# Block 0 of a fused attention and feed-forward kernel: the third chunk's hidden product by one level of Strassen's method, and block 0 in a plan of slots

## The chip, the cores and the metric

The kernel runs on one core of a Trainium2 chip. A core has TensorE (PE, matrix products; its weight loads, PEld, overlap them), VectorE (DVE), ScalarE (ACT), GpSimd (POOL) and SyncE (SP, which here only issues DMA transfers). Each engine works through its own queue in order and waits on semaphores. Matrix products land in PSUM, in banks; everything else works in SBUF. All data here is float32, except that the two weight matrices arrive as float64 and are rounded to float32 on the chip.

The metric is the device time of one execution in microseconds; lower is better. Several runs of the same kernel lie within about 0.15% of each other.

## The reference

```python
kv = np.einsum('bhsd,bhse->bhde', k, v)          # batch 8, heads 8, seq 576, head_dim 64
out = np.einsum('bhsd,bhde->bhse', q, kv)
rms = np.sqrt(np.mean(out * out, axis=-1, keepdims=True) + 1e-06)
attn = (out / rms * g_norm).astype(np.float32)
x = attn.transpose(0, 2, 1, 3).reshape(B * S, H * D)   # 4608 x 512
h = x @ w_in                                     # w_in 512 x 2048
g = np.maximum(0.01 * h, h)
return (g @ w_out).astype(np.float32)            # w_out 2048 x 512
```

## The kernel before

**Blocks and chunks.** The 4608 rows of x are worked on in nine blocks of 512. The 2048 hidden columns come as four chunks (c = 0 to 3) of 512. For each chunk a block computes h = x · w_in (an h product), applies the leaky ReLU to get g, and adds g · w_out to the block's outputs (an o product). Attention for the following block is computed between them.

**Strassen.** A product of 512 x 512 by 512 x 512 taken in halves needs eight quarter products; Strassen's method (in Winograd's form) makes it with seven, and sums of quarters before and after them. `strassen` (line 923) yields after each of the seven, in the order 1, 2, 6, 5, 7, 3, 4. Each has four matrix products of 128x256 columns; on TensorE each of these is two instructions. Products 1, 6, 7 and 4 run in one PSUM bank, 2, 5 and 3 in a second; products 1, 2 and 5 open their bank anew, the others add to what is there, after the engine that read the last state is done. `product_h` (line 995) does this for h: ScalarE copies products 1, 5 and 6 out, VectorE adds products 2, 3 and 7, ScalarE applies the ReLU to each finished quarter, from PSUM for product 4. The sums on the side of w_in are s5, s6 (first pair) and s7, s3 (second pair), made by `sides_w1` (line 776); those on the side of x are t1 to t4, where t3 overwrites a quarter of x. Later blocks use two levels.

**Block 0** is in `first_block` (line 1431). Before the change its chunks 0, 1 and 2 go by plain h products (`plain_h`: per 128 hidden rows four matrix products of 512 columns, in banks ha and hc by turns), and only chunk 3 by one level of Strassen. The outputs of chunks 0 to 2 are plain (`plain_o`, a unit being one 128-row part of one left factor) and collect in four banks of PSUM, which ScalarE copies to SBUF at the end of the block (line 1532). The h product of a chunk stands beside the o products of the chunk before it. The o products of chunk 3 run in block 1.

**Weights.** The 32 weight pieces ("jobs" 0 to 31, 512 KB each as float64) are loaded by SP into seven buffers by turns (`load_w`) and rounded (`round_on`): two conversions on ScalarE, a clamp, a shift, a merge and a final add on VectorE. For jobs in `SIGNED` ScalarE makes the sign part, and VectorE's shift falls away. A job's last steps are issued with the next job's first ones (`end_w`). Before, jobs 0 to 3 are w_in of chunk 0, then w_in of chunk 1 and w_out of chunk 0 take turns, then w_in of chunk 2 and w_out of chunk 1, then w_in of chunk 3, w_out of chunk 2 and of chunk 3.

**Order.** While block 0 is built, nearly all instructions are pinned in program order (`pin`, `lined`); `ROUND_0`, `ROUND_1`, `ROUND_3`, `A_1`, `A_3`, `TAIL_1`, `X_1`, `S_1` and `UNITS` (lines 1422 to 1429) say after which step how many jobs are rounded, which steps of the attention of batch 1 go on, and where sums stand. GpSimd makes block 1's first sums of w_in (`sides_w1(0)`, behind a one-element copy at line 1520 that waits for job 31) and the sums of the fourth chunk's w_out (`sides_w2`, lines 797 to 818). In block 1 `combine` (line 832) makes second-level sums of w_in, parts 0 and 1 on GpSimd and part 2 on VectorE, in the tile `stage`.

Of the kernel before, what the change touches and what calls it, by code (L numbers as in the profile page):

```python
# [25 lines left out]
def kernel(  # L26
# [36 lines left out]
    nc = tc.nc  # L63
# [11 lines left out]
    U = 2  # L75
# [94 lines left out]
    def load_pair(b, p, what="kvq"):  # L170


        if "k" in what:
            k_ins[b, p] = load_two(nc.sync, k[b, 2 * p:2 * p + 2], in_tile("k"))
        if "v" in what:
            v_ins[b, p] = load_two(nc.sync, v[b, 2 * p:2 * p + 2], in_tile("v"))
        if "q" not in what:
            return
        t = q_tile(b, p)
        for l in range(2):  # L180
            for c in range(2):
                r0, n = 64 * l + 32 * c, T * D - 32 * c
                src = q[b, 2 * p + half_of(p, l)].rearrange("(t s) d -> t (s d)", s=T)
                pin(nc.sync.dma_start(t[r0:r0 + 32, :n], src[:, 32 * c:]))
        q_ins[b, p] = t
# [113 lines left out]
    for c in range(NC):  # L299
        for h in range(2):  # L300
            for u in range(U):
# [2 lines left out]
                           (w2_rows(h, c, u), w_out[f0:f0 + P].rearrange("p (v n) -> p v n", v=1 + h))]  # L304

    w_jobs = [w_jobs[8 * c + 2 * i + second] for stage_ in
              (((0, 0),), ((0, 1), (1, 0)), ((0, 2), (1, 1)), ((0, 3),), ((1, 2),), ((1, 3),))
              for i in range(2 * U) for second, c in stage_]
    w_raws = {}
    halved = [j for j, (_, src) in enumerate(w_jobs) if src.shape[1:] == (2, N2)]  # L310
# [16 lines left out]
            pass  # L327

    half_way = collections.deque()
    SIGNED = range(6, len(w_jobs), 2)  # L330

    def end_w():
        while half_way:
# [425 lines left out]

    more_all = consts.tile([P, 19 * P], F32, name="more")  # L760
    more = view(more_all, 0, 19, P)
    later, tick = [], -7

    def put_off(n, what):
        later.append((tick + n, what))
# [2 lines left out]
    def add(eng, out_, a, b_, minus=False, pinned=False):  # L768
        ins = eng.tensor_tensor(out_, a, b_, op=ALU.subtract if minus else ALU.add)  # L769
        if pinned or steady or in_first:  # L770
            pin(ins)
# [1 line left out]
    def w1_sums(c, i):  # L773
        return pair(i, U, 2, 2, P) if c and not in_first else view(more_all, i * NW, U, 2, 2, P)

    def sides_w1(c, eng=nc.gpsimd):


        a11, a12 = w1_sb[0][c][:, :, :2, :], w1_sb[0][c][:, :, 2:, :]
        a21, a22 = w1_sb[1][c][:, :, :2, :], w1_sb[1][c][:, :, 2:, :]  # L780
        s12 = w1_sums(c, 0)
        sides = {1: a11, 2: a12, 4: a22, 5: s12[:, :, :, 0, :], 6: s12[:, :, :, 1, :]}
        add(eng, sides[5], a21, a22)
        add(eng, sides[6], sides[5], a11, True)

        def more():
            s34 = w1_sums(c, 1)
            sides.update({7: s34[:, :, :, 0, :], 3: s34[:, :, :, 1, :]})
            add(eng, sides[7], a11, a21, True)
            add(eng, sides[3], a12, sides[6], True)  # L790
        return sides, more

    w2_dram = [[dram.tile([P, 2, U, N2], F32, name=f"w2_{c}_{i}") for i in range(2)]
# [576 lines left out]
    def go(steps, n=None):  # L1370
        while n is None or n > 0:
            if next(steps, steps) is steps:
                return
            n = None if n is None else n - 1
# [28 lines left out]
    def round_to(n):  # L1403
        nonlocal loaded, rounded
        while rounded < n:
            if loaded < len(w_jobs):
                load_w(loaded)
                loaded += 1
                if loaded in PAIR_AT:
                    load_pair(1, PAIR_AT[loaded])  # L1410
            round_on(rounded)
            rounded += 1
        if n == len(w_jobs):
            end_w()
# [4 lines left out]
        while later and later[0][0] <= tick:  # L1419
            later.pop(0)[1]()  # L1420

    ROUND_0 = 5, 6, 8, 9
    ROUND_1 = 11, 12, 14, 15, 17, 18, 19, 20, 21, 22, 24, 25, 26, 27, 28, 29
    ROUND_3 = 30, 31, 32
    TAIL_1 = 2, 3, 4
    A_1 = 5, 6, 8, 9, 10, 11, 12, 13, 14
    A_3 = 0, 1, 3, 4, 5, 5, 6
    X_1, S_1 = 12, 14
    UNITS = 2, 2, 2, 3, 2, 3, 2

    def first_block():
        x = xTs.pop(0)
        b11, b12 = x[:, :2, :N2], x[:, :2, N2:]
        b21, b22 = x[:, 2:, :N2], x[:, 2:, N2:]
        t1, t2, t4 = xt1[0], xt24[0][:, 0], xt24[0][:, 1]
        lefts = [], [], []

        def plain_h(c, n):
            h, u = divmod(n, U)
            h_ps = ps_m.tile([P, NT], F32, tag=("ha", "hc")[n % 2], name="h_ps")  # L1440
            parts = 2 if c == n == 0 else 1
            for part in range(parts):
                cols = slice(part * NT // parts, (part + 1) * NT // parts)
                for e in range(NE):
                    matmul(h_ps[:, cols], lhsT=w1_sb[h][c][:, u, e, :], rhs=x[:, e, cols],
                           start=(e == 0 and part == 0), stop=(e == NE - 1), skip_group_check=True)
            gT = view(g_all[c % 2], n * NT, NT)
            lefts[c].append([gT[:, t * P:t * P + P] for t in range(4)])
            return lambda: pin(nc.scalar.activation(gT, h_ps, func=AF.Prelu, alpha=SLOPE))

        accs = [ps_m.tile([P, DM], F32, tag=t, name="o_acc") for t in ("oa", "oc", "hb", "hd")]
        os = dict(zip(("11", "21", "12", "22"), o_homes))
        quarters = o_all.rearrange("p (i u n) -> p i u n", i=4, u=2)

        take = []

        def plain_o(c):
            for n, left in enumerate(lefts[c]):
                h, u = divmod(n, U)
                right = w2_rows(h, c, u)  # L1460
                end = c == NC - 2 and n == 2 * U - 1
                for t in range(4):
                    for v in range(1 + h):
                        cols = slice(v * N2, v * N2 + N2) if h else slice(0, NT)
                        matmul(accs[t][:, cols], lhsT=left[t], rhs=right[:, v, :],
                               start=(c == 0 and n == 0), stop=end, skip_group_check=True)
                    if end:
                        to = quarters[:, t // 2::2, t % 2, :]
                        part = accs[t].rearrange("p (v n) -> p v n", v=2)
                        take.append((nc.scalar.copy, to, part))  # L1470
                    yield

        for n in range(2 * U):
            relu_h = plain_h(0, n)
            round_to(ROUND_0[n])
            relu_h()
        tail = tail_of(0, NT, S)
        a_steps = attention(1, False)
        x_adds = (t1, b12, b11, True), (t2, b22, t1, True), (b12, b22, b12, True), (t4, b21, t2, True)
        for c in range(1, NC - 1):  # L1480
            o_steps = plain_o(c - 1)
            for n in range(2 * U):
                for half in range(2):
                    at = 4 * U * (c - 1) + 2 * n + half
                    if half:
                        go(o_steps, 4)
                    else:
                        relu_h = plain_h(c, n)
                    round_to(ROUND_1[at])
                    if not half:  # L1490
                        relu_h()
                    if at in TAIL_1:
                        go(tail, 1)
                    if at in A_1:
                        go(a_steps, 1)
                    if at == X_1:
                        for x_add in x_adds[:2]:
                            add(nc.vector, *x_add)
                    if at == S_1:
                        w_sides, more_h = sides_w1(NC - 1, nc.vector)  # L1500
        x_sides = {1: b11, 2: b21, 3: b22, 4: t4, 5: t1, 6: t2, 7: b12}
        o_steps = plain_o(NC - 2)
        g_sides = {}
        h_steps = product_h(-1, w_sides, x_sides, g_sides)
        for t in range(7):
            later_steps()
            if t < len(ROUND_3):
                round_to(ROUND_3[t])
            go(h_steps, 1)
            if t == 0:  # L1510
                for x_add in x_adds[2:]:
                    add(nc.vector, *x_add)
                more_h()
            go(o_steps, UNITS[t])
            go(a_steps, A_3.count(t))
            if t == 2:
                for p in range(2):
                    load_pair(2, p)
            elif t == 3:
                pin(nc.gpsimd.tensor_copy(more_all[:1, :1], w2_1[:1, 1, NC - 1, U - 1, :1]))  # L1520
                next_sides, more_h = sides_w1(0)
            elif t == 5:
                for i in range(2):
                    sides_w2(-1)[1](i)
                next_x, _, sums, _ = sides_x(1)
                go(sums, 2)
            elif t == 6:
                go(sums)
        more_h()
        go(h_steps)  # L1530
        for copy, to, part in take:
            pin(copy(to, part))
        o_queue.append(product_o(-1, g_sides, os, store(0)))
        return next_sides, next_x
# [173 lines left out]
```

## Time and profile before

| | us |
|---|---|
| median of 3 runs | 905.16 (904.28 to 905.49) |
| the profiled execution | 904.45 |
| its span on the core | 902.7 |
| block 0's h and o products on TensorE, first to last | 22.29 to 122.80 |
| of these, third chunk's h beside the second's o | 65.81 to 95.83 |

Every date in the text is in microseconds from the start of the span. In a line of a timeline stand start, length, engine, line, operation, output and input tiles, count, and in brackets how long the engine had been idle and what ended that. In the chain of waits each line has start, length and the work that the end of the execution hung on. Tiles appear by shortened names: `w_all` is the home of w_in, `w` those of w_out, `pairs`, `more` and `stage` are working space, `xt` the sums on the side of x. Nearly all matrix products carry line 128 and nearly all additions line 769, so they are told apart by tiles.

### The profile page before, as it was taken

To read this page: it belongs to the slowest core of one execution; us is meant where nothing else is said; L and a number is where in the kernel's file an instruction comes from. 1 tells how busy PE (TensorE), PEld (TensorE's weight loads), DVE (VectorE), ACT (ScalarE), POOL (GpSimd) and SP (SyncE) were. 2 spreads that over 40 slices of the span, in tenths; PEclk is the share of its full clock that TensorE was granted. 3 is DMA by queue.
4 is the path that set the end of the run, shared out by engine and by line. 5 is a ranking of instruction groups with operands and counts; after the bars stand their busy time and mean duration, and the time that the engine had idled before them with its cause. 6 is when DMAs were issued, how large, how long until landed. Compare 5 with 4: busy or idle time off the path is not lost.

```text
span 902.7 us, 19186 instructions
## 1 busy us (share of the span) xinstructions
PE 896.1 (99%) x7376; PEld 796.5 (88%) x7376; DVE 620.0 (69%) x947; ACT 340.0 (38%) x661; POOL 529.0 (59%) x675
## 2 busy tenths in 40 slices
PE   9999999999999999999999999999999999999998
PEld 5555688888998999999999999999999999999997
DVE  6988798376675667685967498666876684646453
ACT  5755532232244432434343433343244324222420
POOL 2000189877438774776657584758486847783730
PEclk9999999999999999999999999999999999999999
DMA  8979139967989688968897788858886778677731
GB/s 302 310 232 326 48 116 287 321 241 252 277 281 336 194 273 262 312 206 277 241 313 277 234 278 270 319 176 263 255 279 184 233 217 269 203 234 233 252 118 52
DMA packets 109820, 220.07 MB, mean 244 GB/s; under 512 B 11296, under 2 KB 51616, under 8 KB 109728
## 3 DMA queue, kind: packets, MB, share of 16 engines
q1 hardware_dynamic: 105296, 213.26, 74.3%
q10 hardware_dynamic: 3984, 4.39, 1.4%
q8 instruction: 59, 0.97, 0.4%
q0 software_dynamic: 448, 1.18, 0.3%
q14 instruction: 33, 0.27, 0.1%
HBM read 188.38 MB, written 30.41 MB: 242 GB/s over the span
## 4 chain that ended last, share of the span: by engine, by line
PE 94%; POOL 2%; DMA 1%; DVE 1%; issue 1%; ACT 0%; DVEq 0%; POOLq 0%; ACTq 0%
PE o_a L128 20%; PE o_c L128 16%; PE h_hd L128 10%; PE h_ha L128 9%; PE h_hc L128 9%; PE h_hb L128 9%; PE o_acc L128 5%; PE h_ps L128 5%; PE o_ps L128 3%; PE h_a L128 2%; PE h_c L128 2%; PE h_b L128 2%; PE h_d L128 1%; PE kv_ps L128 1%; DMA pairs<-in_v_dram 1%; POOL more L769 1%
## 5 line engine op out<-in xcount | busy, mean ns | idle before, releaser
L769 POOL TENSOR_TENSOR gs<-g 128x512 f32<-128x512 f32 x64 | 88.0, 1376 | 128.5 <-ACT g L962 61.5
L769 DVE TENSOR_TENSOR o_all<-o_c,o_all 128x256 f32<-128x256 f32 (+1 forms) x128 | 72.1, 563 | 62.3 <-PE o_c L128 47.0
L128 PE MATMUL o_a<-pairs,gs 128*128 128x256 f32 x480 | 113.8, 379 | 0.0
L962 ACT ACTIVATE g<-g 128x512 f32<-128x512 f32 x127 | 77.7, 631 | 75.4 <-DVE g L769 75.3
L769 POOL TENSOR_TENSOR w_all<-w_all 128x512 f32<-128x512 f32 x28 | 49.7, 1775 | 87.1 <-ACT w_all L1184 86.9
L769 DVE TENSOR_TENSOR g<-g,w_all 128x512 f32<-128x512 f32 (+1 forms) x84 | 88.7, 1056 | 14.6 <-POOL w_all L769 8.8
L128 PEld LDWEIGHTS o_a<-pairs,gs 128*128 128x128 f32 x480 | 87.0, 190 | 9.7 <-DVE o_all L769 0.2
L769 POOL TENSOR_TENSOR pairs<-w_all 128x512 f32<-128x512 f32 x6 | 7.9, 1324 | 108.2 <-ACT cut L367 100.6
L769 DVE TENSOR_TENSOR w_all<-h_ha,w_all 128x512 f32<-128x512 f32 x42 | 28.7, 684 | 54.8 <-PE h_ha L128 53.0
L128 PE MATMUL o_c<-pairs,gs 128*128 128x256 f32 x280 | 66.2, 379 | 0.0
L769 DVE TENSOR_TENSOR o_all<-o_a,o_all 128x512 f32<-128x512 f32 (+1 forms) x56 | 37.5, 670 | 39.5 <-PE o_a L128 38.8
L1184 ACT COPY w_all<-h_hc 128x512 f32<-128x512 f32 x42 | 24.8, 591 | 104.2 <-PE h_hc L128 103.9
L1184 ACT COPY w_all<-h_ha 128x512 f32<-128x512 f32 x42 | 24.7, 588 | 104.4 <-PE h_ha L128 104.4
L128 PE MATMUL o_a<-w,g 128*128 128x256 f32 x256 | 60.7, 379 | 0.0
L128 PEld LDWEIGHTS o_c<-pairs,gs 128*128 128x128 f32 x280 | 51.0, 190 | 5.7
L769 DVE TENSOR_TENSOR g<-w_all 128x1024 f32<-128x1024 f32 x28 | 34.9, 1248 | 29.3 <-ACT w_all L1184 29.3
L128 PEld LDWEIGHTS o_a<-w,g 128*128 128x128 f32 x256 | 46.5, 190 | 5.2
L769 POOL TENSOR_TENSOR gs<-gs,g 128x512 f32<-128x512 f32 x32 | 43.8, 1368 | 2.2
L128 PE MATMUL h_hc<-stage,w_all 128*128 128x128 f32 x336 | 44.9, 276 | 0.0
L128 PEld LDWEIGHTS h_ha<-stage,w_all 128*128 128x128 f32 x336 | 43.1, 192 | 1.8 <-POOL xT L769 0.3
L128 PE MATMUL h_ha<-stage,w_all 128*128 128x128 f32 x336 | 44.4, 275 | 0.0
L128 PE MATMUL o_acc<-w,g 128*128 128x256 f32 (+1 forms) x144 | 44.2, 453 | 0.0
(329 smaller groups left out, 2413.8 us busy)
## 6 DMA issues: line engine op xcount, KB each, us to landing
w_all<-w SPq DMA_DIRECT2D x196, 448.0 KB, 4.7
pairs<-w SPq DMA_DIRECT2D x94, 256.0 KB, 4.3
w<-w SPq DMA_DIRECT2D x22, 448.0 KB, 5.4
v_in<-in_v_dram SPq DMA_DIRECT2D x29, 288.0 KB, 5.8
k_in<-in_k_dram SPq DMA_DIRECT2D x28, 288.0 KB, 5.0
q_in<-in_q_dram SPq DMA_DIRECT2D x46, 144.0 KB, 4.8
q_in<-in_q_dram SPq DMA_DIRECT2D x46, 140.0 KB, 4.9
w<-stage SPq DMA_DIRECT2D x12, 512.0 KB, 3.9
```

The source lines that it names most:

```text
L128: pin(nc.tensor.matmul(*args, **kw))
L769: ins = eng.tensor_tensor(out_, a, b_, op=ALU.subtract if minus else ALU.add)
L962: lined(nc.scalar.activation(t, t if src is None else src, func=AF.Prelu, alpha=SLOPE))
L1184: nc.scalar.copy(q[:, at], bank)
```

## The change

The third chunk's h (c = 2) goes by one level of Strassen's method too, by the same `product_h`, beside the o products of chunk 1. Its four quarters of g are then used as plain left factors for the o products of chunk 2, so that no sums of g are made for it. The x sums t1 to t4 serve both chunks and are made earlier; w_in of chunk 2 gets its own four sums on VectorE.

All of block 0 is now told by three strings of slots. In them H is a step of an h product, R the rounding of one more job, E the ReLU of a plain h, T a step of the last rows of batch 0's attention, A a step of batch 1's attention, O the next units of o products, X one x sum, S one pair of w_in sums, Y two x sums of block 1, G the one-element copy on GpSimd, W the w_out sums, L loads. The weight jobs come in another order: w_in of chunk 2 as jobs 12 to 15, ahead of w_out of chunk 1 as jobs 16 to 19. `SIGNED` holds 22 jobs instead of 13.

```diff
     w_jobs = [w_jobs[8 * c + 2 * i + second] for stage_ in
-              (((0, 0),), ((0, 1), (1, 0)), ((0, 2), (1, 1)), ((0, 3),), ((1, 2),), ((1, 3),))
+              (((0, 0),), ((0, 1), (1, 0)), ((0, 2),), ((1, 1),), ((0, 3),), ((1, 2),), ((1, 3),))
...
-    SIGNED = range(6, len(w_jobs), 2)
+    SIGNED = (6, 8, 9, 10, 11, 12, 13, 14, 15, 16, 17,
+              18, 19, 20, 21, 22, 23, 24, 27, 29, 30, 31)
...
-    def sides_w1(c, eng=nc.gpsimd):
+    def sides_w1(c, eng=nc.gpsimd, apart=False):
...
+        if apart:
+            return sides, first, more
+        first()
         return sides, more
...
-    ROUND_0 = 5, 6, 8, 9
-    ROUND_1 = 11, 12, 14, 15, 17, 18, 19, 20, 21, 22, 24, 25, 26, 27, 28, 29
-    ROUND_3 = 30, 31, 32
-    TAIL_1 = 2, 3, 4
-    A_1 = 5, 6, 8, 9, 10, 11, 12, 13, 14
-    A_3 = 0, 1, 3, 4, 5, 5, 6
-    X_1, S_1 = 12, 14
+    PLAN_0 = "HRE THER RHE HRE"
+    PLAN_1 = "HRER RRORT HE OT XRHE OARA RRHEAR XRAO"
+    PLAN_2 = ("SROH RHAO OSXRAH ROHR HO HXSAARO RHRAO "
+              "RRHO RAHO HOLSA RHO HAWAO HAAYGO OYSH")
     UNITS = 2, 2, 2, 3, 2, 3, 2
...
+        sides = [sides_w1(c, nc.vector, True) for c in (2, 3)] + [sides_w1(0, apart=True)]
+        w_sums = [do for _, *two in sides for do in two]
+        relus, o_steps, h_steps, sums, g_sides = [], None, None, None, {}
+        units = itertools.chain([4] * 4, UNITS, UNITS)
...
+        acts = {"R": lambda: round_to(rounded + 1), "E": lambda: relus.pop()(), "T": lambda: go(tail, 1),
+                "A": lambda: go(a_steps, 1), "X": lambda: add(nc.vector, *x_adds.pop(0)),
+                "S": lambda: w_sums.pop(0)(), "Y": x_sums, "G": gate, "W": w_out_sums,
+                "O": lambda: go(o_steps, next(units)),
+                "L": lambda: [load_pair(2, p) for p in range(2)]}
+        for at, what in enumerate(PLAN_0.split()):
+            acts["H"] = lambda: relus.append(plain_h(0, at))
+            for key in what:
+                acts[key]()
+        o_steps = plain_o(0)
+        for at, what in enumerate(PLAN_1.split()):
+            acts["H"] = lambda: relus.append(plain_h(1, at // 2))
+            for key in what:
+                acts[key]()
+        acts["H"] = lambda: go(h_steps, 1)
+        for at, what in enumerate(PLAN_2.split()):
             later_steps()
...
+            c = 2 + at // 7
+            if at % 7 == 0:
+                o_steps = plain_o(c - 1)
+                h_steps = product_h(c - NC, sides[c - 2][0], x_sides, g_sides)
+            for key in what:
+                acts[key]()
+            if at == 6:
+                go(h_steps)
+                g11, g21, g22, g12 = g_of(-2)
+                lefts[2].extend([(g11, g21, g12, g22)[2 * h + t // 2][:, 2 * u + t % 2, :]
+                                 for t in range(4)] for h in range(2) for u in range(U))
+        next_sides = sides[2][0]
+        while w_sums:
+            w_sums.pop(0)()
         go(h_steps)
```

In the fourth chunk's last slot (t = 6) the code before ran a step of the h product and then the last o units (`go(h_steps, 1)`, later `go(o_steps, UNITS[t])`); the new string there is "OYSH". The one-element copy stands in slot 5 instead of 3, and the w_out sums in slot 4 instead of 5.

More of the change, by code (lines that the diff above doesn't have):

```diff
@@ L761 @@
     more = view(more_all, 0, 19, P)
-    later, tick = [], -7
+    later, tick = [], -7 * (NC - 2)
     def put_off(n, what):
@@ L782, in sides_w1, with first @@
         sides = {1: a11, 2: a12, 4: a22, 5: s12[:, :, :, 0, :], 6: s12[:, :, :, 1, :]}
-        add(eng, sides[5], a21, a22)
-        add(eng, sides[6], sides[5], a11, True)
+        def first():
+            add(eng, sides[5], a21, a22)
+            add(eng, sides[6], sides[5], a11, True)
         def more():
@@ L1471, in plain_o @@
                     yield
[L1473 to L1476, printed above, removed]
+        x_adds = [(t1, b12, b11, True), (t2, b22, t1, True), (b12, b22, b12, True), (t4, b21, t2, True)]
+        x_sides = {1: b11, 2: b21, 3: b22, 4: t4, 5: t1, 6: t2, 7: b12}
         tail = tail_of(0, NT, S)
         a_steps = attention(1, False)
-        x_adds = (t1, b12, b11, True), (t2, b22, t1, True), (b12, b22, b12, True), (t4, b21, t2, True)
@@ L1480, in first_block @@
[L1480 to L1505, printed above, removed]
-            later_steps()
[L1507 to L1528, printed above, removed]
@@ L1529, in first_block, with x_sums, gate @@
-        more_h()
+        sides = [sides_w1(c, nc.vector, True) for c in (2, 3)] + [sides_w1(0, apart=True)]
+        w_sums = [do for _, *two in sides for do in two]
+        relus, o_steps, h_steps, sums, g_sides = [], None, None, None, {}
+        units = itertools.chain([4] * 4, UNITS, UNITS)
+        def x_sums():
+            nonlocal sums, next_x
+            if sums is None:
+                next_x, _, sums, _ = sides_x(1)
+            go(sums, 2)
+        def gate():
+            pin(nc.gpsimd.tensor_copy(more_all[:1, :1], w2_1[:1, 1, NC - 1, U - 1, :1]))
@@ new lines, in w_out_sums @@
+        def w_out_sums():
+            for i in range(2):
+                sides_w2(-1)[1](i)
+        next_x = None
+        acts = {"R": lambda: round_to(rounded + 1), "E": lambda: relus.pop()(), "T": lambda: go(tail, 1),
[3 more added lines that the diff above has]
+                "L": lambda: [load_pair(2, p) for p in range(2)]}
```

## The prediction

> **What bounds the kernel.** I read the busy table first, then the waits of TensorE, then the chain of waits with windows over block 0, then the timelines of four engines around the one place that loses time.
>
> ```profile
> span 902.7 us, 19186 instructions
> PE 896.1 (99%) x7376; PEld 796.5 (88%) x7376; DVE 620.0 (69%) x947; ACT 340.0 (38%) x661; POOL 529.0 (59%) x675
> ```
>
> TensorE is busy for 99% of the span. What it waits for by name is 2.9 us in all; only one such wait lies inside the work and is large:
>
> ```profile
> PE idle_ps L128 <- DVE group L378: 1.5, 1, 1.5
> PE h_a L128 <- DVE g L769: 0.9, 1, 0.9
> PE kv_ps L128 <- DMA pairs<-in_v_dram: 0.3, 1, 0.3
> PE h_hd L128 <- ACT w_all L1587: 0.2, 1, 0.2
> ```
>
> So the time moves only if TensorE's own work changes or a wait appears or goes. The chain of waits (start, length, work) gives the prices: a plain h product, one Strassen product, and the end of block 0.
>
> ```profile
> 65.81 3.43 PE h_ps L128 x8
> ...
> 95.83 1.73 PE h_a L128 x8
> ...
> 119.34 1.73 PE h_a L128 x8
> 121.07 1.73 PE o_acc L128 x8
> 122.80 1.73 PE h_a L128 x8
> ```
>
> Windows (length, then busy PE, PEld, DVE, ACT, POOL, clock, DMA share, GB/s): the third chunk's stage is 65.81 to 95.83, the fourth's ends at 122.80. TensorE is full in both, at a granted clock of 1.00, and VectorE nearly so in the second.
>
> ```profile
> 65.81:95.83 30.02, 30.02 (x169) 16.35 (x169) 22.39 (x41) 16.38 (x30) 1.27 (x1) 1.00 0.95 297
> 95.83:122.80 26.97, 26.97 (x121) 19.86 (x121) 24.95 (x38) 12.36 (x25) 12.10 (x10) 1.00 0.01 2
> ```
>
> The 0.9 us wait is early in block 1. Timelines of ScalarE, VectorE, GpSimd and TensorE:
>
> ```profile
> 121.11 0.60 ACT L962 ACTIVATE g<-h_a 128x512 f32<-128x512 f32 x1 [2.35 <-PE h_a L128]
> ...
> 138.37 0.81 DVE L769 TENSOR_TENSOR stage<-w_all 128x128 f32<-128x128 f32 x1
> 139.22 0.77 DVE L769 TENSOR_TENSOR stage<-stage,w_all 128x128 f32<-128x128 f32 x1
> 139.91 1.35 DVE L769 TENSOR_TENSOR stage<-w_all 128x128 f32<-128x128 f32 x1
> 141.19 0.28 DVE L769 TENSOR_TENSOR stage<-w_all,stage 128x128 f32<-128x128 f32 x1
> 142.48 0.67 DVE L769 TENSOR_TENSOR g<-h_a,g 128x512 f32<-128x512 f32 x1
> ...
> 139.80 1.32 POOL L769 TENSOR_TENSOR gs<-g,gs 128x512 f32<-128x512 f32 x1
> ...
> 143.21 1.99 PE L128 MATMUL h_a<-g,w_all 128*128 128x256 f32 x8 [0.94 <-DVE g L769]
> ```
>
> Four equal VectorE adds take 0.28 us when GpSimd stands still and up to 1.35 while it adds. They hold back the add at 142.48, which frees bank ha for product 4 of block 1.
>
> **The change, part by part.**
>
> *Products.* The third chunk's h was 4 x 3.43 = 13.72 us; by seven products it is 7 x 1.73 = 12.11. Its output products and the attention pieces stay, only interleaved otherwise: **-1.61 us**, all on the path. The Trainium skill, "TensorE: Matmul & The Clock Gate", section "Back-to-back issue gap", speaks against it: weight load and multiplication together set the spacing, 81 ns at 128 columns and 131 ns at 512. Its estimate, on a straight line between them, is 56 x 98 ns against 32 x 131 ns, +1.3 us, and the sum below would be +1.1. The rows here disagree: eight instructions of 512 columns take 3.43 us and eight of 256 take 1.73, the same per column.
>
> *The end of block 0.* The plan's last slot is "OYSH": the last output products now stand before product 4 of the fourth chunk, not behind it. Block 1's product 1 opens bank ha anew, and ScalarE must first read product 4 out of it. Before, the 1.73 us of output products at 121.07 hid that (read 121.11 to 121.71). Now nothing does: drain of the last matmul 0.16 (the timeline's 1.89 less the spacing 1.73), 0.04 to ScalarE's start (121.07 to 121.11), 0.60 for the read, 0.06 back (VectorE's add ends 143.15, TensorE starts 143.21): **+0.86 us**; at the least the read alone, 0.60, at the most the 1.10 that the other wait for a freed bank costs (below). Nothing else is in ScalarE's queue then; behind product 1 stands all of block 1 on TensorE, so it is paid in full.
>
> *Work beside the products.* VectorE gains four w_in sums (0.70 each from start to start, 89.86 to 90.57) and three adds from PSUM (0.6 each): +4.6. Jobs whose sign ScalarE does rise from 13 to 22, and each saves VectorE one shift, 0.45 (start to start, 85.94 to 86.39): 9 x 0.45 = -4.05. Net +0.6. ScalarE gains 9 signs and 3 copies at 0.55, +6.6, and idles 8 to 15 us in each window above. Both hide under TensorE as long as nothing below is late. I put them at 0; from below nothing is to be won but the wait named next, from above see the rivals.
>
> *Is anything late in the third chunk?* Order from the diff, lengths from the rows, from 65.81: two output units 1.72, products 1 and 2 at 67.5 and 69.3, four units, product 6 at 74.4, three units, products 5 and 7 at 78.7 and 80.5, two units, product 3 at 83.9, kv, three units, product 4 at 89.7, the fourth chunk at 94.2. Summing VectorE's queue (1.7 us for a signed job, 2.1 for another) puts the two w_in sums at 69, the add that frees hc for product 5 at 74, the t4 sum at 87: 3 to 5 us early each. ScalarE's new copies and relus wait for products and for VectorE's adds, and behind them stand the conversions of jobs 21 to 27, which VectorE's rounding and, through their buffers, SP's loads wait for; with signs at 0.55 and conversions at 1.15 a pair, its copy for product 7 comes at 77.
>
> *SP.* The loads of attention pair (1,2) now stand before job 20, not behind job 22; both wait for kv of block 1, which ends at 58.3 instead of 62.1. From the issue at 62.20 to job 24's landing at 77.17 took 15.0 us for two pair loads and two jobs; with a job more (512 KB at 252 to 297 GB/s, 1.9) job 22 lands at about 75.3. ScalarE reaches it at 74.7. Half a microsecond late, with 3 us to spare before product 7. Cost 0.
>
> *Last rounding and GpSimd.* Job 31 now comes behind the copy after product 6 of the fourth chunk (103.83 - 1.6, done about 105.8 with a relu before it), so ScalarE ends it at 106.9, not 108.0. VectorE's finish came 6.8 us later (108.02 to 114.83); I keep that: 113.7. GpSimd, which waited for it at 114.98, starts 1.2 us earlier, and one of its w_out sums (1.27) no longer waits for job 31 and is done already: 2.5 us ahead. Its add at 139.80 to 141.12 then ends near 138.6. VectorE stays tied to TensorE there (its add at 133.99 waits for o_a), so its two slow 128x128 adds at 139.22 and 139.91 move to 138.5 and 139.2 and meet a still GpSimd: about 0.3 and 1.0 saved. The wait is 1.10 in all (product 4 could start at 140.38 + 1.73 = 142.11, started 143.21): between **0 and -1.10**. I take **-1.10**, as the saving is 1.3; the other end is a rival.
>
> *Sum:* -1.61 + 0.86 - 1.10 = -1.85. The profiled execution took 904.45 (span 902.7 and 1.75 around it), so 902.6; the median of the runs is 905.16, 0.71 above, so **903.3**. From block 1 on the diff moves nothing on TensorE.
>
> **Rivals.**
>
> 1. *The wait in block 1 stays*, because GpSimd gains no lead over TensorE. For it: the 2.5 us hang on one estimated date, 113.7. Against: the w_out sum is freed in any case. -0.75: 904.4.
>
> 2. *VectorE at the end of block 0 becomes the bound: slower.* In the fourth stage it is busy 24.95 of 26.97 us, and the plan adds job 28's rounding there (2.1) and takes two x sums away (1.2): +0.9. A further clash with GpSimd, like that of job 30's last three steps (4.36 us from 108.57 for 1.45 of work), costs 2.9. The victim is product 6 of block 1, which needs the sum t2, done at 126.17 before, by 126.03. Beyond t2 at 126.8 the gain is gone; with both costs t2 is done at 130.0 and TensorE waits 4.0: +3.2, 908.4. Against: the chain to t2 hangs on job 31, which I have 1.1 us earlier.
>
> 3. *The gain is given back in block 1*, where the DMA share is 1.03 from 143 to 180: 905.2. Against: TensorE waits for no transfer there.
>
> 4. *Narrow products cost more per column*: products following other shapes have taken 1.92 instead of 1.73 (100.18). At 1.92 each h saves 0.28: 904.6. The skill's page named above points this way. Against: that row is the exception.
>
> **How the numbers follow.** Forecast 0.50, rivals 0.22, 0.18, 0.07, 0.03. Predicted 903.3; the likeliest case's own range is 902.8 to 904.0 (the run spread, and part of the wait left). The range 902.6 to 905.8 also takes in rivals 1, 3 and 4 and the light end of 2. A measurement can tell 0.2% here, 1.8 us: faster means under 903.35, slower over 906.97. The forecast lies on the first line; 0.30 of it goes below, 0.20 above, as the saving worked out for the wait (1.3) is more than the wait; rivals 1, 3, 4 are "same", and of rival 2 0.13 is beyond 906.97. Faster 0.30, same 0.57, slower 0.13.
>
> **What would show it.** Seven products of 1.73 between 67 and 91 with no idle TensorE; a wait of TensorE on ScalarE's relu of about 0.7 before block 1's first product; the wait on VectorE's g add gone or shrunk, GpSimd idle before 139; block 2 starting some 1.9 us earlier. I am wrong if TensorE waits in the third or fourth chunk, above all product 5 on hc or block 1's product 6 on t2, or if the first output of block 1 waits for a load.

## The result, and the profile after

| | before | after |
|---|---|---|
| median of 7 runs each, us | 905.16 (904.24 to 905.91) | 902.57 (902.00 to 902.94) |
| ratio | | 0.9971, 95% interval 0.9960 to 0.9983 |
| profiled execution, us | 904.45 | 902.06 |
| its span, us | 902.7 | 900.4 |
| first h product | 22.29 | 21.95 |
| the kv group behind product 4 of block 1 (at 164.12 and 161.88), counted from the first h product | 141.83 | 139.93 |
| last group of matrix products (at 898.72 and 896.48), counted from the first h product | 876.43 | 874.53 |
| end of the span, counted from the first h product | 880.41 | 878.45 |

The change makes the kernel 0.29% faster, 2.59 us where 1.85 was worked out. The measured 902.57 lies 0.03 below the low end of the range.

The last three rows of the table are the most useful ones here. A kv group is 72 small matrix products of the attention; block 1 has two, and the one meant here and below is the second, the first behind the place that used to lose time. The first h product starts between 21.95 and 22.37 in all the profiles of this study, for reasons ahead of block 0. Counted from it, two executions of one kernel repeat to less than a tenth of a microsecond through block 0 and most of block 1 (the two pairs below differ by 0.00 and 0.08). So the two traces can be compared to a tenth where the times can't: the change is worth 141.83 - 139.93 = **1.90 us**, all of it before 140 us of work. Behind that the distance stays: 1.90 at the last matrix products too, and 1.96 at the end of the span.

The busy table and the waits of TensorE, of the kernel after:

```profile
span 900.4 us, 19235 instructions
PE 893.8 (99%) x7400; PEld 801.0 (89%) x7400; DVE 622.8 (69%) x945; ACT 345.4 (38%) x673; POOL 529.9 (59%) x675
```

```profile
PE idle_ps L128 <- DVE group L379: 1.5, 1, 1.5
PE h_a L128 <- ACT g L969: 0.7, 1, 0.7
PE kv_ps L128 <- DMA pairs<-in_v_dram: 0.6, 1, 0.6
PE h_hd L128 <- ACT w_all L1588: 0.2, 1, 0.2
```

TensorE still sets the end. Its wait for VectorE's add in block 1 is gone from the list, and a wait for ScalarE's ReLU stands there instead.

The chain of waits (start, length, work) shows the third chunk's products and the end of block 0:

```profile
62.01 5.17 PE o_acc L128 x20
67.18 1.73 PE h_a L128 x8
68.90 1.73 PE h_c L128 x8
...
78.37 1.73 PE h_c L128 x8
80.10 1.73 PE h_a L128 x8
...
89.27 1.73 PE h_a L128 x8
...
119.08 1.74 PE h_a L128 x8
120.82 0.02 issue
120.84 0.61 ACT g L969
121.45 0.04 issue
121.49 2.00 PE h_a L128 x8
```

The windows (length, then busy PE, PEld, DVE, ACT, POOL, clock, DMA share, GB/s) of the third chunk's stage and of the fourth's up to block 1's first product:

```profile
65.46:93.84 28.38, 28.38 (x194) 20.96 (x193) 26.04 (x47) 18.05 (x33) 1.28 (x1) 1.00 0.99 323
93.84:121.49 27.65, 26.97 (x120) 19.54 (x119) 25.90 (x38) 14.71 (x29) 14.12 (x11) 1.00 0.17 56
```

The third chunk's stage took 30.02 and takes 28.38, TensorE is busy in all of it, and each narrow product costs 1.73. In the fourth's stage TensorE is as busy as before, 26.97, and idles 0.68: the read of bank ha by ScalarE, which the chain shows between the last product of block 0 and the first of block 1.

The place in block 1 that used to lose time, in the timelines of VectorE, GpSimd and TensorE after the change:

```profile
136.10 1.48 DVE L770 TENSOR_TENSOR stage<-w_all,stage 128x256 f32<-128x256 f32 x1
137.51 0.28 DVE L770 TENSOR_TENSOR stage<-w_all 128x128 f32<-128x128 f32 x1
137.82 0.29 DVE L770 TENSOR_TENSOR stage<-stage,w_all 128x128 f32<-128x128 f32 x1
138.03 0.29 DVE L770 TENSOR_TENSOR stage<-w_all 128x128 f32<-128x128 f32 x1
138.23 0.28 DVE L770 TENSOR_TENSOR stage<-w_all,stage 128x128 f32<-128x128 f32 x1
...
139.53 0.68 DVE L770 TENSOR_TENSOR g<-h_a,g 128x512 f32<-128x512 f32 x1
...
135.86 1.45 POOL L770 TENSOR_TENSOR gs<-g,gs 128x512 f32<-128x512 f32 x1
140.66 1.42 POOL L770 TENSOR_TENSOR stage<-pairs 128x256 f32<-128x256 f32 x2 [3.36 <-DVE g L770]
...
141.06 1.89 PE L128 MATMUL h_a<-g,w_all 128*128 128x256 f32 x8
```

GpSimd's last `gs` add ends at 137.31, so VectorE's four 128x128 adds meet a still GpSimd and take 0.28 each. The add that frees bank ha ends at 140.21, 0.85 before TensorE comes to product 4 at 141.06.

### The profile page after: what moved, and what is told of

Same layout as the page of the kernel before. It is cut to its first block, busy times and chain, and to the rows that moved or that the text cites. A ratio compares the mean times of both kernels' runs of the same rounds, so it can differ in the third digit from the quotient of the medians.

```text
span 900.4 us, 19235 instructions
## 1 busy us (share of the span) xinstructions
PE 893.8 (99%) x7400; PEld 801.0 (89%) x7400; DVE 622.8 (69%) x945; ACT 345.4 (38%) x673; POOL 529.9 (59%) x675
## 4 chain that ended last, share of the span: by engine, by line
PE 95%; POOL 2%; DMA 1%; DVE 1%; issue 1%; ACT 0%; POOLq 0%; DVEq 0%; ACTq 0%
PE o_a L128 20%; PE o_c L128 16%; PE h_hd L128 10%; PE h_hc L128 9%; PE h_ha L128 9%; PE h_hb L128 9%; PE o_acc L128 5%; PE h_a L128 3%; PE h_ps L128 3%; PE o_ps L128 3%; PE h_c L128 2%; PE h_b L128 2%; PE kv_ps L128 1%; PE h_d L128 1%; DMA pairs<-in_v_dram 1%; POOL more L770 1%
## 5 line engine op out<-in xcount | busy, mean ns | idle before, releaser
L969 ACT ACTIVATE g<-g 128x512 f32<-128x512 f32 x130 | 79.6, 631 | 82.9 <-DVE g L770 82.8
L770 POOL TENSOR_TENSOR gs<-g,gs 128x512 f32<-128x512 f32 x32 | 44.2, 1381 | 0.0
```

The costliest lines, as they stand in the source:

```text
L969: lined(nc.scalar.activation(t, t if src is None else src, func=AF.Prelu, alpha=SLOPE))
```

## The experiments

The questions were: is the 0.34 us earlier start part of the change; which part of the change clears the wait in block 1; what is the exposed bank worth; does the larger set of signed jobs do anything. The first four kernels ran on one chip (before: median 904.66 of 28 runs), the last four on another (before: 904.67 of 22). The kernel before lay between 904.09 and 906.61 in these runs.

| kernel | median us (runs) | ratio to before, 95% | first h product | the kv group, counted from it |
|---|---|---|---|---|
| after_again | 902.58 (11) | 0.9977, 0.9968 to 0.9986 | 22.23 | 139.93 |
| h_before_o | 901.91 (6) | 0.9969, 0.9958 to 0.9981 | 22.34 | 138.99 |
| after_pool_old | 903.16 (11) | 0.9983, 0.9974 to 0.9992 | 22.28 | 139.93 |
| before_pool_new | 903.34 (11) | 0.9984, 0.9975 to 0.9993 | 22.27 | 140.62 |
| h_before_o_2 | 901.62 (5) | 0.9963, 0.9949 to 0.9977 | 22.37 | 139.07 |
| h_before_o_pool_old | 901.98 (6) | 0.9968, 0.9956 to 0.9979 | 21.96 | 139.36 |
| before_o_first | 904.51 (11) | 1.0004, 0.9995 to 1.0012 | 22.12 | 141.91 |
| after_signed_old | 903.48 (11) | 0.9982, 0.9973 to 0.9991 | 22.01 | 140.19 |

**The changed kernel once more** (after_again, no edit).

> The changed kernel once more, beside the kernel before on the same chip. Theory 1: the work of the change is worth -1.61 (products) +0.84 (bank ha exposed at the end of block 0) -1.10 (wait in block 1 gone) = -1.87 us, and the rest of the -2.59 of the medians is the start, whose length differs from run to run: the first h product, at 21.95 us against 22.29 in the two traces so far, begins anywhere within some tenths of both, and from it to the end the trace takes 1.9 us less than the trace of before. Rival A: the early start belongs to the change: first product again near 21.95, and the ratio again near 0.9971. Theory 1 expects a ratio of 0.9979, rival A 0.9971 to 0.9975.

It starts at 22.23 and comes to block 1's kv group at the same 139.93. The 0.34 us by which the first profile started earlier was chance. Far behind, at 571, this execution loses 0.32 us: a weight load of TensorE waits 0.24 there for a sum on GpSimd, which it doesn't in the trace of after.

**The output products behind product 4 again** (h_before_o). Only TensorE's order differs from after.

```diff
-              "RRHO RAHO HOLSA RHO HAWAO HAAYGO OYSH")
+              "RRHO RAHO HOLSA RHO HAWAO HAAYGO HOYS")
```

> The changed kernel, with the last slot of block 0 turned from OYSH to HOYS: product 4 of the fourth chunk stands before the last output products again; only TensorE's order differs. Theory 1: the wait of 0.69 us on ScalarE's relu before block 1's first product is gone, and since VectorE's add that frees bank ha in block 1 ended 0.86 us early, the wait there does not come back: 0.84 us less than the changed kernel, 901.7 where that has 902.6. Rival B: the exposed wait is what gave GpSimd and VectorE the time; then a wait of about 0.8 us on VectorE's g add is back at 140 and the time is the same as that of the changed kernel.

TensorE in the timeline of h_before_o, at block 1's first product and at its product 4:

```profile
119.31 1.89 PE L128 MATMUL o_acc<-w,g 128*128 128x256 f32 x8
121.04 1.89 PE L128 MATMUL h_a<-xT,w_all 128*128 128x256 f32 x8
...
140.50 1.91 PE L128 MATMUL h_a<-g,w_all 128*128 128x256 f32 x8
```

Product 1 follows 1.73 us behind the output products, without a gap, and product 4 does not wait either: 0.94 us less than after at the kv group. So the exposed bank is worth its gap of 0.84 and the slow start of 0.10 behind it, and the wait in block 1 stays away without it. In this one execution 0.56 us is lost again at 278, where TensorE's waits name a v_in load with 0.3.

**The same kernel again** (h_before_o_2, no further edit), to see whether that late load belongs to it.

> The kernel with HOYS in block 0's last slot once more. Its first trace stood 2.84 us before the kernel before in the middle of block 1 (both counted from their first h product) and only 2.3 at the end; 0.56 us went in block 3, at about 255 to 290, with a wait for a load of v there. Theory 1: that is chance, as single waits for a load are in other traces; this trace goes through that stretch in 32.8 us like the others, and ends 2.6 to 2.9 us before the kernel before, counted from the first product. Rival D (the gain is given back to the transfers, since TensorE is further ahead of them): the stretch takes 33.3 us again.

TensorE at product 4 of block 1 in h_before_o_2:

```profile
140.54 1.98 PE L128 MATMUL h_a<-g,w_all 128*128 128x256 f32 x8
```

No wait for a v_in load is on its list; it gains 0.86 on after at the kv group, 0.08 less than h_before_o, since its product 4 starts slowly (1.98) though it has no gap in front. It comes to the load as early as h_before_o and loses nothing there, so the late load is no fixed price of coming early. Two other traces lose time at the same load: h_before_o_pool_old 0.42 and after_signed_old, which comes there later than these, 1.6. This is the fastest version of the study: 0.9963 of before (0.9949 to 0.9977), and its two medians, taken on the two chips, are 0.7 and 1.0 us below the 902.58 of after.

**After, with GpSimd's old order** (after_pool_old). The w_out sums and the one-element copy go back to the slots they had before; TensorE's order is that of after.

```diff
-              "RRHO RAHO HOLSA RHO HAWAO HAAYGO OYSH")
+              "RRHO RAHO HOLSA RHOGS HAAO HAAWYO OYH")
```

> The changed kernel, with GpSimd's work at the end of block 0 in the order of before: the one-element copy that waits for job 31 and the first sums of block 1 in slot 3, the w_out sums after them in slot 5; only GpSimd's order differs. Theory 1 (GpSimd's lead cleared the wait in block 1, 1.3 of its 2.5 us by this order): GpSimd ends its last add there 1.3 us later, near 138.6 instead of 137.3, two or three of VectorE's four 128x128 adds are slow again, and 0 to 0.4 us of the wait is back. Rival B (the exposed wait gave the time): no change, no wait. Rival C (only the order counts, not the earlier job 31): all of the 1.1 us is back.

The timeline of VectorE and TensorE in after_pool_old:

```profile
137.20 1.35 DVE L770 TENSOR_TENSOR stage<-w_all 128x128 f32<-128x128 f32 x1
138.58 0.29 DVE L770 TENSOR_TENSOR stage<-stage,w_all 128x128 f32<-128x128 f32 x1
...
140.29 0.68 DVE L770 TENSOR_TENSOR g<-h_a,g 128x512 f32<-128x512 f32 x1
...
141.40 1.89 PE L128 MATMUL h_a<-g,w_all 128*128 128x256 f32 x8
```

One of the four adds is slow again (1.35), since GpSimd ends 0.76 later, counted from the first product, than after. But VectorE's add still ends at 140.97, 0.43 ahead of product 4. The kv group is at 139.93, to the hundredth as after: GpSimd's new order isn't needed here. Where two or three slow adds were expected, one was slow.

**Before, with GpSimd's new order** (before_pool_new) and nothing else: the w_out sums to slot 4, the one-element copy to slot 5, block 1's first w_in sums to slot 6.

```diff
-            elif t == 3:
-                pin(nc.gpsimd.tensor_copy(more_all[:1, :1], w2_1[:1, 1, NC - 1, U - 1, :1]))
-                next_sides, more_h = sides_w1(0)
-            elif t == 5:
+            elif t == 4:
...
+            elif t == 5:
...
+                pin(nc.gpsimd.tensor_copy(more_all[:1, :1], w2_1[:1, 1, NC - 1, U - 1, :1]))
...
+                next_sides, more_h = sides_w1(0)
```

> The kernel before, with GpSimd's work at the end of block 0 in the order of the changed kernel: w_out sums first, then the one-element copy and the first sums of block 1; only GpSimd's order differs. Theory 1: one w_out sum no longer waits for job 31, GpSimd's last add before VectorE's g add ends at 139.85 instead of 141.12, VectorE's 128x128 add at 139.91 takes 0.3 instead of 1.3, and the wait of 0.94 falls to 0 to 0.2: 0.8 to 1.1 us less than the kernel before. Rival B (the exposed wait of the changed kernel gave the time): the wait stays at 0.9, the time that of before.

The timelines of VectorE, GpSimd and TensorE in before_pool_new:

```profile
138.55 1.24 DVE L769 TENSOR_TENSOR stage<-stage,w_all 128x128 f32<-128x128 f32 x1
139.71 0.28 DVE L769 TENSOR_TENSOR stage<-w_all 128x128 f32<-128x128 f32 x1
...
141.21 0.67 DVE L769 TENSOR_TENSOR g<-h_a,g 128x512 f32<-128x512 f32 x1
...
138.33 1.31 POOL L769 TENSOR_TENSOR gs<-g,gs 128x512 f32<-128x512 f32 x1
...
142.08 1.89 PE L128 MATMUL h_a<-g,w_all 128*128 128x256 f32 x8
```

GpSimd ends 1.46 us earlier than before, counted from the first product; VectorE's add ends at 141.88 and product 4 comes at 142.08 unhindered. The kv group comes 1.21 earlier than before. So GpSimd's order alone is enough too, in a kernel without the third Strassen product.

**The output products behind product 4, and GpSimd's old order** (h_before_o_pool_old). Both parts undone together.

```diff
-              "RRHO RAHO HOLSA RHO HAWAO HAAYGO OYSH")
+              "RRHO RAHO HOLSA RHOGS HAAO HAAWYO HOY")
```

> The kernel with HOYS, and with GpSimd's work at the end of block 0 in the order of before, so that GpSimd's lead is only that of the earlier job 31 and TensorE comes 0.94 us earlier than in the run that kept OYSH with this order. Theory 1 (the wait in block 1 is a race between TensorE and GpSimd's last add beside VectorE's four 128x128 adds): GpSimd ends at 138.4, 0.6 later than with the new order, and a wait of 0.1 to 0.4 us on VectorE's g add is back. Rival E (job 31 alone is enough, whatever TensorE does): no wait. Time: 0 to 0.5 us above HOYS with the new order.

The timelines of VectorE and TensorE in h_before_o_pool_old:

```profile
139.68 0.67 DVE L770 TENSOR_TENSOR g<-h_a,g 128x512 f32<-128x512 f32 x1
...
138.40 1.89 PE L128 MATMUL o_a<-pairs,gs 128*128 128x256 f32 x8
140.40 1.99 PE L128 MATMUL h_a<-g,w_all 128*128 128x256 f32 x8
```

TensorE was ready at 138.40 + 1.73 = 140.13; VectorE's add ended at 140.35, and product 4 started at 140.40. The wait is back, 0.27 us of it, and with the slow first product behind it (below) the kv group comes 0.29 to 0.37 later than in the two runs of h_before_o. That job 31 is done earlier takes away most of the wait, but not all.

**Before, with the output products ahead of product 4** in the last slot (before_o_first). Only TensorE's order differs from before.

```diff
+            if t == 6:
+                go(o_steps, UNITS[t])
...
-            go(o_steps, UNITS[t])
+            if t < 6:
+                go(o_steps, UNITS[t])
```

> The kernel before, with only the last slot of block 0 changed: the last output products stand before product 4 of the fourth chunk, as in the changed kernel. Theory 1: a wait of 0.7 us on ScalarE's relu appears before block 1's first product (0.94 us with the slow restart behind it), and since GpSimd stays where it is while TensorE comes later, the wait of 0.94 in block 1 shrinks to 0.3 to 0.6: in all 0.3 to 0.6 us more than the kernel before. Rival B (the exposed wait alone clears the other): the wait in block 1 is gone, and the time is 0 to 0.3 us less than before.

The timelines of TensorE and VectorE in before_o_first:

```profile
123.32 1.99 PE L128 MATMUL h_a<-xT,w_all 128*128 128x256 f32 x8 [0.69 <-ACT g L962]
...
141.16 1.89 PE L128 MATMUL o_a<-pairs,gs 128*128 128x256 f32 x8
143.12 1.99 PE L128 MATMUL h_a<-g,w_all 128*128 128x256 f32 x8
...
142.39 0.68 DVE L769 TENSOR_TENSOR g<-h_a,g 128x512 f32<-128x512 f32 x1
```

TensorE loses its 0.94 at the end of block 0, and the old wait shrinks from 1.10 to 0.23 (ready at 141.16 + 1.73 = 142.89, started at 143.12). In all the kv group moves by 0.08, where a loss of 0.3 to 0.6 was expected, and the time not measurably (ratio 1.0004, 0.9995 to 1.0012). A stall earlier on the same engine nearly pays for itself, because it gives GpSimd and VectorE the time that they lacked later.

**After, with the old set of signed jobs** (after_signed_old).

```diff
-    SIGNED = (6, 8, 9, 10, 11, 12, 13, 14, 15, 16, 17,
-              18, 19, 20, 21, 22, 23, 24, 27, 29, 30, 31)
+    SIGNED = range(6, len(w_jobs), 2)
```

> The changed kernel with the 13 signed jobs of before: VectorE makes nine more shifts (4.05 us), ScalarE nine signs less. Theory 1 (VectorE's extra work hides; it idles 0.5 to 1.9 us in five places between 40 and 96 in the trace of the changed kernel, and of the nine shifts only 0.45 net fall between 96 and the add that frees hc for product 5 of the fourth chunk, which was 0.7 us early): no new wait of TensorE in block 0; job 31 is done 0.9 later, GpSimd with it, and 0 to 0.2 us of the wait in block 1 is back. Time within 0.3 us of the changed kernel. Rival 2 of the prediction (VectorE bounds the end of block 0): waits on VectorE of 1 us or more before block 1's product 6 or the fourth chunk's product 5.

The timelines of VectorE and TensorE around the fourth chunk's product 5, and a line from TensorE's waits, in after_signed_old:

```profile
104.57 0.68 DVE L769 TENSOR_TENSOR g<-h_c,g 128x512 f32<-128x512 f32 x1
...
105.30 1.99 PE L128 MATMUL h_c<-xt,more 128*128 128x256 f32 x8
```

```profile
PE o_ps L128 <- DMA v_in<-in_v_dram: 1.3, 1, 1.3
```

VectorE is later by its shifts. Its add that frees bank hc ends at 105.25, where the product before is out of TensorE's way at about 105.18, so product 5 waits 0.12 and starts slowly: the kv group comes at 140.19 instead of 139.93. No wait in block 0 was expected. In after, the same add ends at 104.38 and product 5 starts at 105.11, so with the new set of signed jobs there is 0.7 us to spare here, and the set is worth 0.26 us of time. The rest of this execution's distance to after, 1.6 us, is lost at 280, where TensorE waits 1.3 for a load of v_in.

**All runs of the wait in block 1 together.** The dates count from the first h product: the end of GpSimd's last `gs` add, the end of VectorE's add that frees bank ha, and when TensorE had its previous product behind it. Room is how far VectorE's add ends ahead of TensorE.

| kernel | GpSimd's add ends | VectorE's add ends | TensorE ready | room |
|---|---|---|---|---|
| before | 118.83 | 120.86 | 119.82 | -1.04 |
| before_o_first | 118.70 | 120.95 | 120.77 | -0.18 |
| before_pool_new | 117.37 | 119.61 | 119.81 | 0.20 |
| h_before_o_pool_old | 116.15 | 118.39 | 118.17 | -0.22 |
| h_before_o | 115.46 | 118.03 | 118.16 | 0.13 |
| h_before_o_2 | 115.53 | 118.10 | 118.17 | 0.07 |
| after_pool_old | 116.12 | 118.69 | 119.12 | 0.43 |
| after | 115.36 | 118.26 | 119.11 | 0.85 |
| after_again | 115.36 | 118.26 | 119.12 | 0.86 |
| after_signed_old | 116.97 | 119.22 | 119.35 | 0.13 |

It is a race. TensorE waits where the room is negative, and by that amount and some 0.05 us more. Little room costs a little as well: product 4 takes 1.98 us with 0.07 of room and 1.91 or 1.92 with 0.13, where it takes 1.89 with 0.20 and more. Put alone into the kernel before, GpSimd's new order brings 1.24 us of room and TensorE's own stall 0.86. The earlier job 31 did not run alone: h_before_o_pool_old has it together with the rest of the change (the third Strassen product, the larger set of signed jobs), and stands 0.82 above before. Of the three only the order is enough without one of the others. Two pairs ran, and both are enough: order and job 31 in h_before_o, job 31 and the stall in after_pool_old. The three don't add up: with the third Strassen product TensorE comes 1.6 earlier too, so h_before_o has no more room than before_pool_new, and at 0.13 and 0.07 its two traces stand close to the edge.

## Why the prediction came out as it did

*The terms of the sum were right.* The products were put at -1.61 and measured -1.64 (the windows, 30.02 to 28.38). The bank at the end of block 0 was put at +0.86: the trace after has TensorE's last product at 118.92, ready for the next at 118.92 + 1.73 = 120.65, and started at 121.49, which is 0.84. To it comes 0.10 for a slow start, since the product behind a wait takes 2.00 where one without takes 1.89. The wait in block 1 was put at -1.10, and it took its slow start of 0.10 with it: -1.20. The sum is -1.64 + 0.94 - 1.20 = -1.90, against -1.85, and the traces show 1.90. Both slow starts were left out of the working, and by luck they cancel.

*The step that failed* is the last one, "the median of the runs is 905.16, 0.71 above, so **903.3**". It took the distance of a median of three runs to the profiled execution for a property of the kernel. With 28 and 22 runs, on two chips, the kernel before has medians of 904.66 and 904.67, 0.2 above its profiled 904.45. The two profiled executions of the changed kernel lie 0.51 below and 0.08 above its medians, so this distance is no constant. The sum by itself, 904.45 - 1.85 = 902.6, is what the changed kernel takes: medians of 902.57 and 902.58. That it meets them to a few hundredths is in part luck, for 904.66 less the 1.90 of the traces is 902.76. Measured in one set beside 28 runs of before, the gain is 904.66 - 902.58 = 2.08; the 2.59 of the first comparison is larger by the 0.5 that its seven runs of before lay higher. The 0.2 between 2.08 and 1.90 is well inside the interval of that comparison (1.3 to 2.9 us).

*The low end of the range failed with it.* It was 902.6, which is the worked sum with nothing below it: neither the spread of a median (seven runs of after lie between 902.00 and 902.94) nor a term that is larger than taken. The spread is wider than three runs of before let it seem: its 28 runs lie between 904.09 and 906.61, 0.28% and not 0.15%. With 0.71 added to the forecast, this looked like room and was none. By the prediction's own line, 903.35, the result is faster, and it gave that 0.30 against 0.57 for the same. This came from the shift too: the line lay 0.05 above the forecast, and 0.75 above the sum.

*The reason for the cleared wait was right and not the only one.* The forecast named two causes, job 31's earlier date (113.7; it was 113.02) and the w_out sum no longer behind it, and put GpSimd's last add at 138.6, 2.5 us earlier than before. It ended at 137.31, and counted from the first h product that is 3.5 earlier. What the forecast did not name is the third cause, TensorE's own stall at the end of block 0. Its dates held the stall (it moved VectorE's adds by 0.7, which is 1.61 less 0.86), but the text gave it no part in clearing the wait. The stall brings 0.65 to 0.72 us of room in the changed kernel (after_pool_old against h_before_o_pool_old, after against h_before_o). That is why undoing GpSimd's order costs nothing in after_pool_old, and why the two terms +0.86 and -1.10 are not independent: before_o_first shows that in the kernel before the first of them would have taken 0.87 of the second along.

*Rivals.* The first, that the wait stays, did not come: the room is 0.85. The second, VectorE as the bound at the end of block 0, did not come either: t2 is done at 122.83 and needed at 125.74. Its place is real, though. With the old signed jobs the fourth chunk's product 5 does wait for VectorE, which costs a quarter of a microsecond and not several. The third, time given back in block 1, is out, as the distance between the traces stays at 1.90 through its end. The fourth, dearer narrow products, is out: each takes 1.73 throughout the third chunk. The estimate worked out from the Trainium skill's page "TensorE: Matmul & The Clock Gate", section "Back-to-back issue gap", +1.1 us in all, does not hold for these float32 products.

*What the forecast took for granted in the third chunk held.* TensorE does not idle in it, the work added to VectorE (25.90 of 27.65 us busy in the fourth stage) and to ScalarE stays covered, although VectorE's busy time over the whole execution grew by 2.8 us (620.0 to 622.8) where 0.6 was reckoned, and the loads moved past job 20 make nothing late.

## What to carry to other kernels

Work a sum against one profiled execution and leave it there: a median of three runs says where the runs scatter, not how far the next kernel's median lies from its profile. Where one engine sets the end, a stall that is added ahead of a wait is not simply added: first ask how much time it gives the engines that the later wait is for. And a bank that changes from one stage to the next is best opened behind other products: moving two output units back behind the last product, a change of one letter's place in a plan, was worth another 0.9 us in the trace here.

## What the runs showed of the hardware

- **TensorE restarts slowly after a wait, and after small products.** The first matrix instruction behind a wait takes 483 ns where the others take 379, and the group of eight 1.99 to 2.00 us instead of 1.89. So each of these waits cost 0.10 us more than its gap shows, and the wait of 0.12 in after_signed_old costs nearly twice that. A wait is not needed for it: in every trace here the group behind the small products of attention, such as the one at 126.78 in before, starts with 483 ns too, without a wait for another engine. Of the kernel before, the shortest, median and longest instruction of each group (ns), and where it lies:

```profile
L128 PE MATMUL h_a<-xT,w_all x8: 379/379/379, 122.6 to 124.1; 128*128 128x256 f32 x8
L128 PE MATMUL h_a<-xt,more x8: 379/379/483, 126.8 to 128.4; 128*128 128x256 f32 x8
L128 PE MATMUL h_a<-g,w_all x8: 379/379/483, 143.2 to 144.8; 128*128 128x256 f32 x8
```

- **One execution is nearly a copy of another.** Counted from the first h product, after and after_again agree to 0.01 us at the kv group. The traces differ because the start moves by 0.4 us, because single loads come late (0.26 and 1.29 us of waiting), and once because of a sum on GpSimd (0.24).
- **Such late loads may decide medians.** The eleven times of after_signed_old fall into four at 902.28 to 902.54, one at 903.01 and six at 903.48 to 904.09; in after_again three of eleven lie in the upper group. One profile, that of after_signed_old, caught an execution with a v_in load 1.3 us late. Whether every time in the upper groups is such a load, and why after_pool_old and after_signed_old fall there more often than after does, was not settled: their positions in blocks 0 and 1 explain 0.0 and 0.26 us of the 0.6 and 0.9 that their medians lie higher.
